# The second eviction and transpose of a left unit moved behind the sum and the mix of its segment

## The chip, the cores and the metric

The kernel runs on one core of one Trainium2 chip. The metric is the device time of one execution in microseconds; of three runs the median is 1787.72 us (1786.72 to 1793.3). All times below are microseconds of the device unless a unit is named. In the text PE is the matrix engine, DVE the vector engine, ACT the scalar engine, POOL the general-purpose engine, and SP the engine that, in the part of the kernel that matters here, issues every DMA.

## What is computed

Two branches are mixed by a gate, over one sequence of 2048 rows of 640 elements in bf16:

```
g = sigmoid((x * gate_w).sum(-1))
a: for s in range(64):                          # segments of 32 rows, in sequence
       h = concat([mem, x[32*s : 32*s+32]])     # 8 memory rows + 32 rows = 40
       q, k, v = h Wq, h Wk, h Wv               # 32 heads of 192
       p = softmax(mask(q k^T / sqrt(192)))
       o = (p v) Wo                             # 40 rows of 640
       mem = o[:8];  a[s] = o[8:]
b = (gelu(x w_gate) * (x w_up)) w_down
out = g * a + (1 - g) * b
```

The 64 segments are a recurrence: the first eight output rows of a segment are the memory of the next one, so no projection of the next segment can start before the sum of this one is transposed back.

## The kernel before

**Stages.** First comes branch b for all rows (until about 180 us), which also leaves x and b in DRAM scratch. Then come 64 segments of about 25 us each. They are all straight-line code: every engine has one list of instructions, written in the order in which the Python program records them, and a recording layer adds semaphore waits for each pair that touches the same memory. Nothing is reordered later, so each engine works through its list and a waiting instruction holds up all that stands behind it on that engine. For SP that means: a DMA whose data isn't ready holds up every DMA recorded after it.

**Main rows and left rows.** A segment has 40 rows. Only 32 of them fit a block of columns: the eight memory rows and the first 24 rows of x. The last eight x rows of each segment are called left rows. Those of four segments make 32 rows, a group; their Q and K don't depend on the memory, so they are projected ahead of time in `left units`. There is one unit for each group and octet of heads (8 heads; four octets): five steps `("lf", place, u, k)` of eight matmuls, one half for Q and one for K, into two PSUM banks. Then follow two eviction steps `("le", place, u, m)`, m = 0 for Q and m = 1 for K. `left_evac` makes of each: an ACT copy from PSUM to a row buffer (`left_rows`, L920), a DVE 32x32-block transpose of the row buffer into the store buffer `lst[3]` (L922), and after the K half one SP DMA of 192 KB from `lst[3]` to the scratch `left_qk_scratch` (`left_store`, L926). Later `stg_load` (L971) brings the left rows of a segment back, 96 KB at a time, and POOL copies them into the Q and K tiles (`left_fill`, L977 and L979).

**Places.** `PROGS` has one list of steps for each of the four segments of a group; segment s runs list s % 4, called its place here. Place 0 has one left unit, place 1 two, place 2 one, place 3 none (it has other extra work: the values of left rows, and the output projection of the left rows). The steps at the end of a list are `("pv", 3)`, the probabilities times the values for the last octet, and `("wo", 3, 0)`, `("wo", 3, 1)`, the last 48 matmuls (L1275) of the output projection.

**The end of a segment.** When the list is through, `segment` records, in this order: the two halves of the sum Z (DVE, L1429) each followed by its transpose back into the input tile of the next segment (DVE, L1433), then `mix` (DVE, L1021, with POOL's L1014 and L1019 ahead of it), then the deferred evictions (`post`), then `stg_load(s + 1, 1)` on SP. An `le` step whose position in its list is behind `("wo", 3, 1)` is deferred; the others are recorded where they stand:

```python
if n > n_wo:
    post.append(item[2:] + (n,))
else:
    left_evac(s, *item[2:], n)
...
mix(s)
...
for i in post:
    left_evac(s, *i)
...
    stg_load(s + 1, 1)
```

The position also picks the row buffer (`spare_rows`): ahead of `("wo", 3, 1)` it is the second value buffer for both halves, so the second ACT copy has to wait until the first transpose has read it; behind it, the row buffer lies in the K tile, which POOL's L979 of the next segment writes.

**Weights.** The weights don't all fit on chip. Sixteen slots of memory are shared by two pieces each: 13 of Q, K and V (384 KB) and three of Wo (480 KB). When PE has used a piece of the first octet, SP loads the piece of the last octet of the same segment over it (`swap_loads`, L630), in the order K piece 0, Q pieces 2 to 4, K pieces 1 to 4, V pieces 0 to 4, and three of Wo when `("wo", 0, 0)` and `("wo", 0, 1)` are through. The pieces are used in the same segment: Q and K of the last octet at about 10 to 15 us, V at 17 to 20, and Wo by the last 48 matmuls. The next segment swaps them back in the same way, so each segment loads 6.6 MB.

Of the kernel before, what the change touches and what calls it, by code (L numbers as in the profile page):

```python
# [231 lines left out]
def _build(nc, A_x, A_mem0, A_Wq, A_Wk, A_Wv, A_Wo, seg_len, w_gate, w_up, w_down,  # L232
# [271 lines left out]
    def piece_view(key, o):  # L504
        if key[0] == 3:
# [975 lines left out]
def bass_gated_mix__memory_aug_recurrent_mem_tr__glu_gated_geglu__prompt_kernel(  # L1481
    nc,
    A_x,
    A_mem0,
    A_Wq,
    A_Wk,
    A_Wv,
    A_Wo,
    A_seg_len,
    B_x,  # L1490
    B_w_gate,
    B_w_up,
    B_w_down,
    gate_w,
    out,
):
    _build(nc, A_x, A_mem0, A_Wq, A_Wk, A_Wv, A_Wo, A_seg_len, B_w_gate, B_w_up, B_w_down, gate_w, out)
# [33 lines left out]
```

## Time and profile before

| what | value |
|---|---|
| median of three runs | 1787.72 us |
| the profiled execution, its own time | 1784.35 us |
| its span, first to last instruction | 1782.5 us |
| granted clock of PE | 0.999 |
| PE busy | 1626.4 us, 91% |
| DVE, ACT, POOL busy | 54%, 45%, 18% |
| DMA | 500.22 MB, mean 281 GB/s |

The profiled execution is 3.4 us below the median of the runs.

The trace was cut at the end of the last L1275 matmul of each segment. The next table gives means over the segments of each place (segments 1 to 59; 14 of place 0 and 15 of each other). "Start" is the end of L1275 of the segment before, all times are from there, and a row tells of the segment that then runs.

| | place 0 | place 1 | place 2 | place 3 |
|---|---|---|---|---|
| segment time, start to the end of its L1275 | 24.91 | 25.46 | 23.59 | 25.89 |
| first projection matmul (L1092) | 0.67 | 0.64 | 1.11 | 1.47 |
| first weight load issued (K piece 0) | 1.21 | 3.07 | 1.67 | 2.13 |
| the same, landed | 4.53 | 6.71 | 5.54 | 5.77 |
| last V piece landed | 18.57 | 20.80 | 19.11 | 19.34 |
| last Wo piece landed | 22.46 | 25.01 | 22.81 | 23.10 |
| from there to the segment's end | 2.45 | 0.46 | 0.78 | 2.79 |

How to read it: what stands at the end of place 0's list shows in the column of place 1, and so on round; the column of place 0 follows the end of place 3, which has no left unit. In place 1 the end of the segment comes 0.43 or 0.44 us after the last Wo piece in 13 of 15 segments; in place 2 it comes at most 0.49 us after it in eight of 15.

### The profile page before, as it was taken

How to read it: one execution, taken by the hardware profiler on the slowest of the kernel's cores; microseconds unless marked ns; L12 is line 12 of the kernel's file. 1: busy time of each engine (PE TensorE's matmuls, PEld its weight loads, DVE VectorE, ACT ScalarE, POOL GpSimd, SP SyncE). 2: the span in 40 equal slices, each digit the busy share in tenths (PEclk: the TensorE clock that was granted, in tenths of full speed). 3: DMA queues.
4: the chain of work that ended last, by engine and by line, in shares of the span. 5: the costliest groups of instructions: out<-in, count | busy, mean ns of one | idle time of the engine just before them, and what ended most of it. 6: DMA issues, size and time to landing. Idle time of an engine off the chain costs nothing. (4 is left out here: it accounts for less than half of the span.)

```text
span 1782.5 us, 80354 instructions
## 1 busy us (share of the span) xinstructions
PE 1626.4 (91%) x39181; PEld 820.6 (46%) x31501; DVE 959.1 (54%) x2939; ACT 800.6 (45%) x1899; POOL 321.0 (18%) x1099
## 2 busy tenths in 40 slices
PE   9999989999899999898999999898989989898987
PEld 4554444444444444454444444454444444454444
DVE  2223655555565655555555655555555555555554
ACT  3222444544444444444444544444444444444443
POOL 1100111121111121111112112121212111111221
PEclk9999999999999999999999999999999999999999
DMA  9814887887778787888788886878778886888786
GB/s 322 292 48 166 314 303 255 321 292 285 278 285 316 278 306 258 306 305 299 273 277 294 310 307 247 311 274 324 272 267 292 299 291 237 313 294 304 270 299 243
DMA packets 265695, 500.22 MB, mean 281 GB/s; under 512 B 99688, under 2 KB 126592, under 8 KB 265344
## 3 DMA queue, kind: packets, MB, share of 16 engines
q1 hardware_dynamic: 262360, 492.03, 77.3%
q8 instruction: 276, 4.52, 1.0%
q10 hardware_dynamic: 2984, 3.05, 0.5%
q14 instruction: 75, 0.61, 0.1%
HBM read 473.88 MB, written 21.11 MB: 278 GB/s over the span
## 5 line engine op out<-in xcount | busy, mean ns | idle before, releaser
L1092 PE MATMUL ps<-arena 128*32 128x384 bf16 x9940 | 734.4, 328 | 61.4 <-DVE arena L1433 50.4
L226 PE MATMUL ps<-arena 128*32 128x384 bf16 x7680 | 586.7, 326 | 13.3 <-ACT arena L920 6.6
L1092 PEld LDWEIGHTS ps<-arena 128*32 128x32 bf16 x9940 | 255.5, 96 | 417.4 <-issue 254.1
L1126 DVE STREAM_TRANSPOSE arena<-arena 128x384 bf16<-128x384 bf16 x512 | 279.1, 564 | 230.6 <-ACT arena L1112 230.1
L1112 ACT ACTIVATE arena<-ps 128x384 bf16<-128x384 f32 x512 | 236.2, 489 | 180.2 <-PE ps L1092 171.9
L1252 PE MATMUL ps<-arena 128*32 128x320 bf16 x6144 | 295.8, 299 | 16.3 <-issue 16.2
L1252 PEld LDWEIGHTS ps<-arena 128*32 128x32 bf16 x6144 | 164.3, 96 | 76.8 <-issue 26.0
L1170 ACT ACTIVATE ps<-ps 104x160 f32<-104x160 f32 x256 | 74.1, 290 | 245.4 <-DVE ps L1160 245.4
L1158 DVE TENSOR_REDUCE arena<-ps 104x4 f32<-104x160 f32 x256 | 83.2, 325 | 187.0 <-PE ps L1146 187.0
L1208 ACT ACTIVATE arena<-ps 128x448 bf16<-128x448 f32 x192 | 104.8, 546 | 143.9 <-PE ps L1195 143.9
L977 POOL COPY arena<-arena 128x96 bf16<-128x96 bf16 x256 | 69.6, 272 | 535.2 <-PE ps L1146 427.2
L1242 POOL COPY arena<-arena 128x96 bf16<-128x96 bf16 x256 | 68.9, 269 | 496.5 <-ACT arena L1234 397.9
L1115 ACT ACTIVATE arena<-ps 128x384 bf16<-128x384 f32 x256 | 124.9, 488 | 63.2 <-PE ps L1092 63.1
L1234 ACT ACTIVATE arena<-ps 128x480 bf16<-128x480 f32 (+1 forms) x256 | 138.2, 540 | 28.4 <-PE ps L1225 23.6
L1223 PE MATMUL ps<-arena 128*64 128x160 bf16 x1536 | 121.9, 243 | 8.1 <-ACT arena L1115 1.0
L1223 PEld LDWEIGHTS ps<-arena 128*64 128x64 bf16 x1536 | 80.5, 109 | 94.5 <-ACT arena L1208 45.6
L915 PE MATMUL ps<-arena 128*32 128x384 bf16 x1280 | 111.5, 329 | 1.5 <-issue 1.3
L1225 PE MATMUL ps<-arena 128*64 128x64 bf16 x1536 | 104.7, 193 | 5.4 <-issue 5.4
L1172 DVE TENSOR_REDUCE arena<-ps 104x4 f32<-104x160 f32 x256 | 81.7, 319 | 51.6 <-ACT ps L1170 43.1
L922 DVE STREAM_TRANSPOSE arena<-arena 128x384 bf16<-128x384 bf16 x128 | 73.8, 577 | 58.8 <-ACT arena L920 55.5
L1160 DVE TENSOR_TENSOR ps<-ps,arena 104x160 f32<-104x160 f32 x256 | 85.1, 332 | 8.8
L1275 PE MATMUL ps<-arena 128*32 128x160 bf16 x3072 | 72.8, 234 | 13.1 <-DMA arena<-in_A_Wo_dram 7.2
(85 smaller groups left out, 1815.4 us busy)
## 6 DMA issues: line engine op xcount, KB each, us to landing
arena<-in_A_Wk_dram SPq DMA_DIRECT2D x335, 384.0 KB, 7.1
arena<-in_A_Wv_dram SPq DMA_DIRECT2D x335, 384.0 KB, 9.1
arena<-in_A_Wo_dram SPq DMA_DIRECT2D x205, 480.0 KB, 6.9
arena<-in_A_Wq_dram SPq DMA_DIRECT2D x209, 384.0 KB, 5.3
left_qk_scratch<-arena SPq DMA_DIRECT2D x64, 192.0 KB, 2.2
arena<-left_qk_scratch SPq DMA_DIRECT2D x126, 96.0 KB, 2.3
ffn_b_scratch<-arena ACTq DMA_DIRECT2D x16, 160.0 KB, 3.4
arena<-ffn_b_scratch SPq DMA_DIRECT2D x64, 40.0 KB
```

The lines of the kernel that those rows point to most:

```text
L226: return e.add_instruction(mybir.InstMatmult(name=nm, start_tensor_calc=like["start"], stop_tensor_calc=stop, tile_size=(128, 32), tile_po ...
L915: fns.append(lambda e, outp=outp, rhs=rhs, j=j: e.matmul(outp, lhs, rhs, start=(k == 0), stop=(k == KT - 1), tile_position=(0, 32 * j)))
L1092: fns.append(lambda e, outp=outp, rhs=rhs, j=j: e.matmul(outp, lhs, rhs, start=(k == 0), stop=(k == KT - 1), tile_position=(0, 32 * j)))
L1112: S_.add("act", lambda e, m=m, bk=bk: e.activation(out=rows_sb[m], in_=ps[:, bk, 0:384], func=ACTF.Copy), reads=[r_ps[bk]], writes=[r_rows ...
L1115: S_.add("act", lambda e, i=i, bk=bk: e.activation(out=v_sb[i % NVB].rearrange("p (c n) -> p c n", c=3), in_=ps[:, bk, 0:384].rearrange("p ...
L1126: S_.add("dve", lambda e: e.transpose(out=dst[:, :, 0:L], in_=rows_sb[m].rearrange("p (c r) -> p c r", r=L)), reads=[r_rows[m]], writes=[r ...
L1160: S_.add("dve", lambda e: e.tensor_tensor(out=S3, in0=S3, in1=mxb, op=ALU.subtract), reads=[rb, rst], writes=[rb], name="smax sub")
L1208: S_.add("act", lambda e: e.activation(out=PT, in_=ps[:, bank, 0:PTW + 128], func=ACTF.Copy), reads=[r_ps[bank]], writes=[r_PT], name="pT ...
L1223: return [lambda e: e.matmul(full, v[:, e0:e0 + 64], PTm[:, i], start=True, stop=False, tile_position=(0, 64 * i), skip_group_check=True), ...
L1225: lambda e: e.matmul(part, vl[:, e0:e0 + 64], PTl[:, i], start=False, stop=True, tile_position=(0, 64 * i), skip_group_check=True)]
L1234: S_.add("act", lambda e: e.activation(out=apx(u[:, 0, 0, :], [[R, na], [3 * R, 4], [1, R]]), in_=ps[:, A, 0:na * W].rearrange("p (c t r) ...
L1252: fns.append(lambda e, i=i, t=t, j=j, gv=gv: e.matmul(ps[32 * j:32 * j + 32, bank, 0:2 * DJ].rearrange("p (h n) -> p h n", h=2), lhs2[i], ...
```

## The change

At places 1 and 2 the step `("le", place, 1, 1)`, the eviction of the K half of the left unit u = 1, is moved behind `("wo", 3, 1)`, the last step of the list, where place 0 has it. Before, it stood ahead of both `wo` steps at place 1 and between them at place 2.

```diff
@@ place 1
-         ("wo", 2, 1), ("pv", 3), ("lf", 1, 1, 3), ("lf", 1, 1, 4), ("le", 1, 1, 0), ("le", 1, 1, 1), ("wo", 3, 0),
-         ("wo", 3, 1)],
+         ("wo", 2, 1), ("pv", 3), ("lf", 1, 1, 3), ("lf", 1, 1, 4), ("le", 1, 1, 0), ("wo", 3, 0), ("wo", 3, 1),
+         ("le", 1, 1, 1)],
@@ place 2
-         ("lf", 2, 1, 2), ("pv", 3), ("lf", 2, 1, 3), ("lf", 2, 1, 4), ("le", 2, 1, 0), ("wo", 3, 0),
-         ("le", 2, 1, 1), ("wo", 3, 1)],
+         ("lf", 2, 1, 2), ("pv", 3), ("lf", 2, 1, 3), ("lf", 2, 1, 4), ("le", 2, 1, 0), ("wo", 3, 0), ("wo", 3, 1),
+         ("le", 2, 1, 1)],
```

It takes effect in 15 groups (the last group has no left unit to prepare), so in 30 segments. In the program that comes of it, no instruction is added or taken away. PE, ACT, POOL and SP have their instructions in the same order as before. On DVE the transpose L922 of the K half now stands behind the two halves of Z, their transposes and the mix. The row buffer of that half changes to the one in the K tile, so its ACT copy no longer waits for the transpose of the Q half, and POOL's L979 of the next segment now waits for the moved transpose. The store L926 still stands on SP ahead of `stg_load` and of the next segment's weight loads, and still waits for the transpose.

## The prediction

> **What bounds the kernel now.** I read the page's first part, then who waits for whom, then the end of a place-0 and of a place-1 segment in the timeline, then the waits on the weight loads.
>
> PE is busy for 1626.4 of 1782.5 us at a granted clock of 0.999, so what there is to win lies in its pauses. The waits (waiter, releaser, total us, times, longest):
>
> ```profile
> PEld ps L1092 <- DVE arena L1433: 77.8, 126, 2.0
> ...
> DVE arena L922 <- ACT arena L920: 55.5, 90, 1.2
> ...
> PE ps L1092 <- DVE arena L1433: 50.4, 48, 1.8
> ...
> ACT arena L920 <- DVE arena L922: 24.4, 30, 1.1
> ```
>
> Those of L1092 are the pause at the 63 segment ends: the next projection waits for the transposed memory. The other two are the left unit's evictions waiting for each other, 30 times: the K half's copy for the Q half's transpose. Next the end of a place-1 segment, engine by engine (start, duration, engine, line; in brackets idle time and releaser):
>
> ```profile
> 828.02 0.39 PE L1275 MATMUL ps<-arena 128*32 128x160 bf16 x12 [0.17 <-DMA arena<-in_A_Wo_dram]
> ...
> 829.76 0.35 PE L1092 MATMUL ps<-arena 128*32 128x384 bf16 x4 [1.35 <-DVE arena L1433]
> ...
> 828.71 0.58 DVE L922 STREAM_TRANSPOSE arena<-arena 128x384 bf16<-128x384 bf16 x1 [0.68 <-ACT arena L920]
> 829.21 0.21 DVE L1429 TENSOR_TENSOR arena<-ps,arena 128x64 bf16<-128x64 f32 x1
> ...
> 829.32 0.37 SPq L926 DMA_DIRECT2D left_qk_scratch<-arena  x1
> 829.79 0.45 SPq L971 DMA_DIRECT2D arena<-left_qk_scratch  x1
> 830.31 0.42 SPq L630 DMA_DIRECT2D arena<-in_A_Wk_dram  x1
> ```
>
> PE ends at 828.42, but Z (L1429) starts only when the second L922 is through, at 829.21: 1.35 us of pause. The same end at place 0, which has the order that the change makes:
>
> ```profile
> 804.28 0.35 PE L1092 MATMUL ps<-arena 128*32 128x384 bf16 x4 [0.63 <-DVE arena L1433]
> ...
> 803.70 0.25 DVE L1429 TENSOR_TENSOR arena<-ps,arena 128x64 bf16<-128x64 f32 x1
> ...
> 804.89 0.57 DVE L922 STREAM_TRANSPOSE arena<-arena 128x384 bf16<-128x384 bf16 x1
> 806.58 1.04 DVE L1126 STREAM_TRANSPOSE arena<-arena 128x384 bf16<-128x384 bf16 x2 [1.12 <-ACT arena L1112]
> ...
> 805.49 0.38 SPq L926 DMA_DIRECT2D left_qk_scratch<-arena  x1
> 805.90 0.51 SPq L971 DMA_DIRECT2D arena<-left_qk_scratch  x1
> 806.45 0.45 SPq L630 DMA_DIRECT2D arena<-in_A_Wk_dram  x1
> ```
>
> The pause is 0.63, but against the segment's end (803.65) the store leaves at 1.84 and the first weight load at 2.80; in the place-1 case they leave at 0.90 and 1.89. Last, who waits for the weight loads (L630):
>
> ```profile
>   PEld ps L1092: 11.8, 22
>   PEld ps L1275: 11.7, 21
>   PE ps L1275: 7.2, 14
> ```
>
> So the loads already end last in some segments. The table of places in the profile section says where: in all of place 1 and half of place 2 the last Wo piece lands 0.43 to 0.49 us before the segment ends.
>
> **The change, part by part.** It acts in 30 segment ends, 15 of place 1 (the segment that follows runs place 2) and 15 of place 2 (then place 3).
>
> *Z and the memory transpose come earlier.* The first projection after places 1 and 2 now comes at 1.11 and 1.47 us (means); after place 0, with the new order, at 0.64. PE gains 0.47 and 0.83 us an end, at most 15 x 0.47 + 15 x 0.83 = 19.5 us. This is the whole of the gain.
>
> *The K half's copy and transpose.* The copy (ACT, 0.49 us) loses its wait for the Q half. The transpose (0.57) runs from 1.24 to 1.81 after the end, within DVE's idle time: 1.12 us are left over in the row of L1126 above. Both cost nothing; were that cover gone, the next Q and K transposes would start up to 0.57 later.
>
> *POOL.* L979 waits for the moved transpose. After place 0 it runs at 805.52 for 0.27 and the first score matmuls follow at 807.49, 1.7 us later. It costs nothing, as the L977 before it comes earlier too; a delay beyond that 1.7 would go to the scores one for one.
>
> *SP, the part that costs.* The store waits for the moved transpose. Behind it on SP stand the stage load L971, needed only at the third octet, and the sixteen weight loads. After place 0 the first weight load leaves at 3.07 us on average (2.8 where nothing else holds it), after places 1 and 2 now at 1.67 and 2.13. So the loads leave 1.40 and 0.94 us later against the segment's end, while PE wants them 0.47 and 0.83 us sooner. The loads are a stream without pause: in the trace undisturbed pieces land 0.97 us apart, and from the first to the last landing it takes 17.27 us in place 2. How far the later issue moves the landings isn't shown for places 2 and 3, so it is bounded. From below: place 3's first load leaves 0.92 later than place 0's and its last Wo piece lands 0.64 later, a share of 0.70; that makes 0.98 and 0.66. From above: place 1, the one place that has the new order ahead of it, lands its last V piece 1.69 and 1.46 later than places 2 and 3. Its first piece lands 1.17 and 0.94 later. I take the middle of what place 1 shows for first and last, 1.43 and 1.20, as it is the same mechanism and part of the upper figure may be place 1's own, with its second left unit.
>
> Place 2: the last Wo piece lands at 22.81 + 1.43 = 24.24, the segment ends 0.44 later (the tail where the loads bind) at 24.68, against 23.59 now: +1.09, times 15 = **+16.4 us**. Ends: 0.98 gives +0.64 or +9.6 us; 1.69 gives +1.35 or +20.3. PE's own path, 23.59 - 0.47 = 23.12, no longer decides.
>
> Place 3 has time at its end (2.79), but not in the middle: the trace has K pieces 2 and 3 of the last octet landing on average 1.28 and 1.21 us before PE uses them. PE 0.83 earlier and loads 1.20 later make 2.03; a wait of 2.03 - 1.21 = 0.82 opens and eats the 0.83: 15 x -0.01, **about 0**. Ends: 0.66 gives 0.83 + 0.66 - 1.21 = 0.28, net -0.55 or -8.3 us; 1.46 gives 1.08, net +0.25 or +3.8. The last Wo piece keeps 2.32 - 2.03 = 0.29.
>
> Places 0 and 1 keep what stands ahead of them: 0.
>
> Sum: 16.4 - 0.1 = **+16.3 us**, ends +1.3 and +24.1. Against the profiled execution's own 1784.35 that is 1800.6; this execution is 3.4 below the median of the runs, and on the median, 1787.72 + 16.3 = **1804.0 us**, slower by 0.9%.
>
> **A rule beside it.** What decides is whether the stream can go faster once it starts later. The rows: 12 x 384 KB and 3 x 480 KB, 6.19 MB, in 17.27 us are 359 GB/s, and 0.97 us a piece is 405 GB/s; the rest are hiccups that every place has. The Trainium skill, page "DMA: Bandwidth & Descriptors", section "Specifications", puts the fabric's ceiling at 435 GB/s; an estimate from that page is 14.2 us for those bytes. At this pace place 2's loads would land by 6.71 + 14.2 = 20.9 and bind nothing, and the sum would be the whole gain, -19.5 us, the first rival below taken to its end; by the rows it is +16.3. No segment of this trace comes near that pace.
>
> **The rivals.**
>
> *The loads still come in time, and it gets faster.* The place is the weight stream of place 2; it decides at a stream (first issue to last landing) of 23.59 - 0.44 - 3.07 = 20.08 us, below which place 2 gains. For it: early loads wait for PE to use the old pieces, and that part of the stream could close up; place 3 shows a share of 0.70 only. Against it: the stream is 21.14 us on average in place 2, 20.30 at the least, and 21.94 in place 1, where the loads leave late. Price: with landings where they are now, place 2 ends at 22.81 + 0.44 = 23.25, -0.34, and place 3 gains its 0.83 whole: 15 x -0.34 + 15 x -0.83 = -17.5, so 1770.2 us.
>
> *Gain and loss cancel.* The share of 0.70 holds: +1.3, 1789.0 us. For it: rows of two places in the same run. Against it: place 1 has the very order and shows more than the full shift.
>
> *The store gets into the stream.* It moves 192 KB out of idle DMA time into the first weight loads. Place 1 has such a store in mid-stream: its third Wo piece lands 1.81 after the second, place 2's 1.25 after, so 0.56 for a store. On top of 1.40 and 0.94 that makes 1.96 and 1.50: place 2 +1.62, place 3 0.83 + 1.50 - 1.21 - 0.83 = +0.29, times 15 = +28.7, 1816.4 us. Against it: after place 0 the store stands there already, and the first piece still lands 3.6 us after its issue, like the others.
>
> That the change does nothing is out: the order on DVE and the waits of store and copy differ in the built program.
>
> **How the numbers follow.** Half a per cent, 8.9 us, is about what a measurement of this kernel tells from no change. The forecast has a chance of 0.64, 0.08 of it below +8.9 us; the first rival 0.13 (0.01 of it within half a per cent), cancelling 0.13, the store in the stream 0.10. Slower: 0.56 + 0.10 = 0.66; within: 0.08 + 0.13 + 0.01 = 0.22; faster 0.12. The forecast's own range is that of the sum's ends, 1789 to 1812. For 8 in 10 it reaches to the cancelling case and to the store's, 1787 to 1816; what is left out is the faster rival and a little above.
>
> **What would show it.** PE's waits for L1433 should fall from 77.8 to about 58 us (77.8 - 19.5), and L920's waits for L922 should vanish; the first matmul after places 1 and 2 comes at 0.64, the store at 1.84, the first weight load at 2.8 to 3.1. PE's waits for L630 should about double. Place 2 takes 24.7 us with a tail of 0.44 in nearly all segments, place 3 25.9 with waits at its K pieces, places 0 and 1 what they take now. I am wrong if place 2's stream falls to 20 us, or if place 3's K pieces are still there when PE wants them.

## The result, and the profile after

The changed kernel takes a median of 1799.49 us against 1786.88 for the kernel before in the same series (eight runs each): a ratio of 1.0064, with a 95% interval of 1.004 to 1.0088, so slower by 0.6%, 12.6 us by the medians. The profiled execution took 1795.71 us, with a span of 1793.7; before it was 1784.35 and 1782.5.

The waits of the changed kernel (waiter, releaser, total us, times, longest), with those that answer to the lines shown of before. PEld is the load of a matmul's first operand into PE; in the lines below that is 32 columns of the segment's own rows and not a weight piece, but it stands ahead of its matmul, so a wait for a weight piece shows on PEld as well as on PE:

```profile
PEld ps L1092 <- DVE arena L1433: 58.1, 126, 0.9
...
PEld ps L1092 <- DMA arena<-in_A_Wk_dram: 45.4, 65, 2.3
...
DVE arena L922 <- ACT arena L920: 37.4, 66, 1.1
...
PEld ps L1092 <- DMA arena<-in_A_Wv_dram: 33.9, 54, 1.4
PE ps L1092 <- DVE arena L1433: 30.7, 48, 0.7
```

The pause at the segment ends fell from 77.8 to 58.1 us, as the change does it, and the longest from 2.0 to 0.9. The wait of L920 for L922 fell from 24.4 us in 30 waits to 6.4 in seven, a row further down in that view: of the 30, 25 stood at the ends of places 1 and 2 and are gone; the seven belong to the other left unit of place 1 (u = 0), which the change doesn't touch and which had five of the 30. In their stead stand waits of the projections for the K and V pieces, which came to 11.8 us in 22 waits on PEld before (79.2 in 119 now). The view of the weight loads (L630) says the same from the other side: who waited for them.

```profile
  PEld ps L1092: 79.2, 119
  PE ps L1092: 40.2, 65
  PEld ps L1275: 17.3, 28
  PE ps L1275: 11.4, 25
```

The end of the same place-1 segment that the prediction showed, engine by engine (start, duration, engine, line, idle time and releaser; this segment ends at 836.27):

```profile
835.87 0.39 PE L1275 MATMUL ps<-arena 128*32 128x160 bf16 x12 [0.56 <-DMA arena<-in_A_Wo_dram]
836.91 0.35 PE L1092 MATMUL ps<-arena 128*32 128x384 bf16 x4 [0.64 <-DVE arena L1433]
...
836.32 0.25 DVE L1429 TENSOR_TENSOR arena<-ps,arena 128x64 bf16<-128x64 f32 x1 [0.90 <-PE ps L1275]
...
837.51 0.58 DVE L922 STREAM_TRANSPOSE arena<-arena 128x384 bf16<-128x384 bf16 x1
...
838.11 0.37 SPq L926 DMA_DIRECT2D left_qk_scratch<-arena  x1
838.53 0.51 SPq L971 DMA_DIRECT2D arena<-left_qk_scratch  x1
839.08 0.45 SPq L630 DMA_DIRECT2D arena<-in_A_Wk_dram  x1
```

Z now starts 0.05 us after the end and PE goes on after 0.64; the moved transpose ends at 838.09, the store leaves at 1.84 from the end and the first weight load at 2.81, where they left at 0.90 and 1.89 before. By place, in means as in the table of before (15 segments; start is the end of the segment ahead):

| | place 1 | place 2 | place 3 |
|---|---|---|---|
| segment time, before / after | 25.46 / 25.32 | 23.59 / 24.67 | 25.89 / 25.73 |
| first projection matmul | 0.64 / 0.64 | 1.11 / 0.64 | 1.47 / 0.64 |
| first weight load issued | 3.07 / 2.98 | 1.67 / 3.23 | 2.13 / 2.93 |
| last V piece landed | 20.80 / 20.65 | 19.11 / 20.56 | 19.34 / 20.75 |
| last Wo piece landed | 25.01 / 24.86 | 22.81 / 24.23 | 23.10 / 24.46 |
| from there to the segment's end | 0.46 / 0.45 | 0.78 / 0.43 | 2.79 / 1.27 |

Place 0 stays at 24.9. In place 2 the last Wo piece now lands 0.43 or 0.44 us before the end in all 15 segments: loads set its end. 15 x 1.08 of place 2, 15 x -0.16 of place 3 and 15 x -0.14 of place 1 make 11.7 us, and the spans differ by 11.2.

### The profile page after: what moved, and what is told of

It is laid out like the page before. It is cut to its first block, busy times and chain, and to the rows that moved or that the text cites. A ratio compares the mean times of both kernels' runs of the same rounds, so it can differ in the third digit from the quotient of the medians.

```text
span 1793.7 us, 80324 instructions
## 1 busy us (share of the span) xinstructions
PE 1636.6 (91%) x39181; PEld 815.7 (45%) x31501; DVE 959.7 (54%) x2939; ACT 797.7 (44%) x1899; POOL 319.3 (18%) x1099
## 5 line engine op out<-in xcount | busy, mean ns | idle before, releaser
L1252 PE MATMUL ps<-arena 128*32 128x320 bf16 x6144 | 292.3, 302 | 7.4 <-issue 7.3
L1252 PEld LDWEIGHTS ps<-arena 128*32 128x32 bf16 x6144 | 162.3, 97 | 61.8 <-issue 12.4
L922 DVE STREAM_TRANSPOSE arena<-arena 128x384 bf16<-128x384 bf16 x128 | 73.5, 575 | 38.4 <-ACT arena L920 37.4
```

The lines of the kernel that those rows point to most:

```text
L1252: fns.append(lambda e, i=i, t=t, j=j, gv=gv: e.matmul(ps[32 * j:32 * j + 32, bank, 0:2 * DJ].rearrange("p (h n) -> p h n", h=2), lhs2[i], ...
```

## The experiments

The theory: the store waits on SP for the moved transpose, sixteen weight loads wait behind the store, and in places 2 and 3 the loads end last. Rivals: the moved transpose costs through POOL's L979; PE merely runs ahead of loads that come when they came; or the transposes' order is worth nothing. The kernel before took medians of 1778 to 1781 us on the chips of these series, less than the 1787 of the first series, so every kernel is given as its ratio to the runs of before of its own series. All eleven kernels had at least five runs. Their times by place are from one profiled execution each, which lay up to 9 us from the median of its kernel, so 0.2 us at a place can be chance (the two profiled executions of the changed kernel differ by 0.18 in place 2 and in place 3).

### The wait on SP alone

DVE and ACT keep the order of before; only the store waits for the mix as well (`r_bz` is what the mix writes, and `left_store` takes it as a further tile to wait for).

```diff
-        if m:
+        if m and u == 1 and s % 4 in (1, 2):
+            pend.append(unit(s, u))
+        elif m:
             left_store(*unit(s, u), 3)
...
         mix(s)
...
+        if pend:
+            left_store(*pend.pop(), 3, [r_bz])
...
         if s + 1 < NSEG:
             stg_load(s + 1, 1)
```

> The order on DVE and ACT is that of the kernel before; at places 1 and 2 only the store L926 is made to wait for the mix (L1021) as well, so it leaves at about the same time as in the changed kernel, and with it everything behind it on SP. Theory (the store holds up the weight loads): the first weight load of places 2 and 3 leaves at about 2.8 to 3.1 us instead of 1.67 and 2.13; place 2 gets 0.8 to 1.1 us longer, place 3, whose projections start no sooner, 0 to 0.2; in all 12 to 18 us slower than before (+0.7% to +1.0%), which is more than the changed kernel loses. Rival (the loss comes from PE running ahead of the loads, or from POOL's wait for the moved transpose, and SP has no part in it): within 3 us of before.

Measured 1.0097 [1.0077, 1.0118], 1796.83 against 1777.77 us. An end of place 1 in this kernel, where line numbers from 1344 on are four higher (L1433 is Z, L1437 its transpose); it ends at 837.72:

```profile
839.30 0.35 PE L1092 MATMUL ps<-arena 128*32 128x384 bf16 x4 [1.57 <-DVE arena L1437]
...
838.25 0.58 DVE L922 STREAM_TRANSPOSE arena<-arena 128x384 bf16<-128x384 bf16 x1 [0.63 <-ACT arena L920]
838.75 0.21 DVE L1433 TENSOR_TENSOR arena<-ps,arena 128x64 bf16<-128x64 f32 x1
...
839.63 0.34 DVE L1021 SCALAR_TENSOR_TENSOR arena<-arena 128x160 bf16<-128x160 bf16 x1
...
840.00 0.37 SPq L926 DMA_DIRECT2D left_qk_scratch<-arena  x1
840.42 0.51 SPq L971 DMA_DIRECT2D arena<-left_qk_scratch  x1
840.97 0.45 SPq L630 DMA_DIRECT2D arena<-in_A_Wk_dram  x1
```

The transposes stand as before, and the store's data is ready at 838.83, but the store leaves at 840.00, when the mix (L1021) is through. The first weight load comes at 2.99 on average in place 2, which takes 24.76 us, 1.17 more than before. So the wait on SP alone makes the whole loss and more; the rival without SP has fallen. Place 3 did not get longer, as I had expected, but shorter (25.57); its first projection comes at 0.98 instead of 1.47, which the next experiment explains.

### One place at a time

The change at place 1 alone, and at place 2 alone.

> The change at place 1 alone. Theory: place 2, the segment after it, loses what it lost in the changed kernel, 1.08 us, and nothing else moves: +16 us (+0.9%). Rival (a cost of the moved transpose itself, the same at both places): half the loss of the changed kernel, about +6 us.

> The change at place 2 alone. Theory: place 3 starts 0.83 us sooner and gives nearly all of it back at the K pieces of the last octet, as in the changed kernel: -2 us, within 4 us of before. Rival (a cost of the moved transpose itself, the same at both places): about +6 us.

Place 1 alone: 1.0048 [1.003, 1.0066], 8.5 us by the ratio. Place 2 alone: 0.9991 [0.9977, 1.0006]. The loss is all place 1's, which is the segment of place 2; a cost of the transpose itself, alike at both, is out. But the change at place 1 alone loses only half of the 16 us that I expected. Place 2 does take 24.51 us, 0.92 more than before (23.51 in the kernel with place 2 alone, on the same chip). What I had not seen is that place 3 gains though nothing was changed at its head: it takes 25.31, its first projection comes at 1.02 (1.47 before) and its first load at 1.69 (2.13). While PE waits for Wo at the end of place 2, ACT and DVE go on with the left unit: its second transpose ends 0.55 us after the segment's end, against 0.99 before. A late end hides part of the next pause.

### The whole change once more

> The changed kernel as it is, on the chip and beside the runs of before that the experiments had, so that the parts can be added up on one chip. Theory: the sum of place1_only (+0.48%) and place2_only (-0.09%), so +0.2% to +0.7%. Rival (the two places work on each other): outside that.

1.0082 [1.0068, 1.0097]; this series ran on another chip than the two parts. It is above their sum, 0.39%, and above the upper end that I gave, though the first series of the same kernel, 0.64% [0.40, 0.88], is not clear of that sum. That the places work on each other is seen in the traces, by the way just told: with place 1 changed, the pause ahead of place 3 is down to 1.02 already, so the change at place 2 wins 0.38 us there and not 0.83, and still pays for the later loads: place 3 takes 25.55 here (25.73 in the first series) against 25.31 with place 1 alone.

### POOL's wait

The deferred K half gets back the row buffer that it had, so that L979 does not wait for the moved transpose.

```diff
-    def left_evac(s, u, m, n):
-        left_rows(*unit(s, u), m, lb[u, m], lst[3], r_lst[3], *spare_buf(spare_rows(PROGS[s % 4], n)))
+    def left_evac(s, u, m, n, buf=None):
+        left_rows(*unit(s, u), m, lb[u, m], lst[3], r_lst[3], *spare_buf(spare_rows(PROGS[s % 4], n) if buf is None else buf))
...
-            left_evac(s, *i)
+            left_evac(s, *i, 1 if q else None)
```

> The changed kernel, but the deferred K half of places 1 and 2 keeps the row buffer that it had before (the second value buffer), so POOL's L979 of the next segment does not wait for the moved transpose, while its ACT copy waits for the first transpose again. Theory (SP alone): as slow as the changed kernel, +0.5% to +0.8% against before, place 2 at 24.6 us. Rival (POOL's wait costs part of it): at least 0.3% better than the changed kernel.

1.0053 [1.0035, 1.0071], place 2 at 24.39 us with its first load at 3.21. The 24.39 is from the fastest of its twelve runs, 9 us below their median, and the ratio is 0.1% below the changed kernel's first one and 0.3% below its second, so the times alone don't rule out a small part. The trace does for the first scores: L979 now ends 1.78 us after the start of place 2 and not 2.20, yet the first product of Q and K (L1141) starts at 4.04 in both kernels. A few tenths of a per cent anywhere else are not ruled out.

### The store behind the V loads

The stores of places 1 and 2 are kept back as above, and sent in the next segment:

```diff
             swap_loads(s, item)
+            if item == ("g", 1, KT - 1) and pend:
+                left_store(*pend.pop(), 3)
```

> The changed kernel, but the two stores of places 1 and 2 are recorded on SP behind the last V load of the next segment, so no weight load waits for the moved transpose. Theory: the pause stays 0.64 us, the first weight load of places 2 and 3 leaves at about 1.2 to 1.6; place 2 gains 0.4 to 0.8 us against before and place 3 its 0.83 whole: 18 to 24 us faster than before (-1.0% to -1.3%), about 30 us faster than the changed kernel. Rival (POOL's wait, the row buffer, or PE running ahead of the loads): as slow as the changed kernel, +8 to +15 us.

> DVE and ACT in the order of the kernel before, the two stores of places 1 and 2 moved behind the last V load as in late_store_12. It differs from late_store_12 by the changed order of the transposes alone, with the loads free in both. Theory: in late_store_12 place 2 was held by its last Wo loads and place 3 by PE, so the order is worth little in place 2 (0 to 0.2 us) and its 0.83 us in place 3: this kernel is 13 to 16 us slower than late_store_12, about 4 us slower than before (0 to +0.4%). Rival (the gain of late_store_12 comes from the loads alone and the order of the transposes is worth nothing): as fast as late_store_12, -0.7%.

With the changed order: 0.9933 [0.9913, 0.9952]. With the order of before: 1.0011 [0.9992, 1.003]. Freeing the loads turns the changed order from a loss of 0.6% into a gain of 0.7%, but it is less than the 1.0 to 1.3% that I expected. The first load of place 2 does leave at 1.18, yet place 2 takes 23.65 us, no less than before (this is the slowest of its six runs, 7 us above their median, so the true figure may be lower): the store now stands in mid-stream, and the first Wo piece lands 1.81 us after the last V piece (1.23 before), which gives back 0.58. Place 3, with 2.4 us in hand at its end, keeps its gain (25.26). The second kernel, slower by 0.8% than the first, shows that the gain is the order's: moving these stores alone wins nothing. Part of what the order gives is the loads' own start: in the second kernel they leave at 1.71 and 1.68 us and not at 1.18, because the first load follows the first projection by about 0.54 us wherever nothing else holds it (1.17 and 1.14 here, 0.64 in the first kernel).

### The store early in the stream, and on the queue of ACT

The first is the kernel of the section above with all three places and `("g", 0, 3)` for the position, behind the third weight load. The other leaves the store where it was and lets ACT issue it, at all three places and, in a second version, at places 1 and 2 alone:

```diff
-            left_store(*unit(s, u), 3)
+            left_store(*unit(s, u), 3, "act" if u == 1 else None)
```

> The changed kernel, with the store of all three places recorded on SP behind the third weight load of the next segment, so that the transpose is long done when SP comes to it. Theory: the first weight load leaves at 1.2 us after each end; place 1 loses its wait for loads (0.5 to 1.2 us less than 25.3), place 2 comes near 23.4, place 3 near 25.2; the store takes up to 0.58 us of the stream. In all 15 to 30 us faster than before (-0.9% to -1.7%). Rival: no faster than late_store_12 (-0.7%), if place 1 is held by something other than the late loads.

> The changed kernel, with the store of all three places issued by ACT, recorded where it was. SP no longer waits for the transpose; ACT does, in its idle time after the segment's end, and issues at about 1.84. Theory: loads as in early_store_012, and the 192 KB move while the first loads are still on their way: 20 to 32 us faster than before (-1.1% to -1.8%). Rival (ACT's issue delays its next row copies, which the first scores need): no faster than early_store_012, with the first scores later by what the issue takes.

> The changed kernel with the stores of places 1 and 2 issued by ACT, place 0 left as it was: the change with the wait on SP taken out of it and nothing else improved. Theory: place 2 as in act_store_012 (23.2 us, -0.4), place 3 too (25.1, -0.8), place 1 as before (25.4): 15 to 20 us faster than before (-0.8% to -1.1%), and slower than act_store_012 by the 0.9 us of place 1 times 15. Rival (most of the gain of act_store_012 is place 0's): within 0.3% of before.

> The order of the kernel before, with the stores of all three places issued by ACT. It differs from act_store_012 by the changed order of the transposes alone, with the loads leaving at 1.2 to 1.7 us in both. Theory: the order is worth 0.8 us at place 3 and 0.2 to 0.5 at place 2, so this kernel is 14 to 20 us slower than act_store_012 (-0.5% to -0.9% against before). Rival (with the loads free the order is worth nothing): as fast as act_store_012, -1.7%.

| kernel | ratio to before [95%] | place 1, 2, 3, us |
|---|---|---|
| early in the stream, all places | 0.9858 [0.9836, 0.988] | 24.51, 23.25, 25.12 |
| on ACT, all places | 0.9834 [0.981, 0.9857] | 24.56, 23.21, 25.06 |
| on ACT, places 1 and 2 | 0.9894 [0.9876, 0.9913] | 25.18, 23.15, 25.12 |
| on ACT, all places, order of before | 0.9963 [0.995, 0.9976] | 24.47, 23.60, 25.87 |

The end of place 1 with the store on ACT (it ends at 816.09):

```profile
816.73 0.35 PE L1092 MATMUL ps<-arena 128*32 128x384 bf16 x4 [0.64 <-DVE arena L1433]
...
816.14 0.32 SPq L971 DMA_DIRECT2D arena<-left_qk_scratch  x1
817.27 0.33 SPq L630 DMA_DIRECT2D arena<-in_A_Wk_dram  x1
...
817.93 0.37 ACTq L926 DMA_DIRECT2D left_qk_scratch<-arena  x1
818.43 0.87 ACT L1112 ACTIVATE arena<-ps 128x384 bf16<-128x384 f32 x2 [2.67 <-PE ps L1092]
```

The stage load no longer waits behind the store, the first weight load leaves at 1.18, and the store goes out at the same 1.84 without holding up either. ACT's next row copy comes at 2.34, as it did after place 0 in the kernel before (805.98 - 803.65 = 2.33), so the delay that the rival named is not there. Its median of 1751.71 us against 1780.61 is the lowest of all, 1.7% faster than before and, by the two ratios to before, some 2.3% faster than the changed kernel. What the changed order is worth with the loads free is the distance of the last row from the second: 1.3%, where the pause was 0.64 instead of 1.59 and 1.57 us. The lesser half of the gain is place 0's: 0.6% between the second and the third row. Both distances compare ratios of two series on two chips; by the places of the profiled executions the order wins 0.39 us in place 2 and 0.81 in place 3, 18 us or 1.0%.

The last row misses what I expected of it (-0.5% to -0.9%): it is 0.4% faster than before. I had the loads leave at 1.2 to 1.7 us in both kernels; with the order of before they leave at 2.13 and 2.12 in places 2 and 3, again 0.54 behind the first projection. So the 1.3% is the pause and the earlier start of the loads together. The store early on SP and the store on ACT can't be told apart by their times (medians of 1753.91 and 1751.71, intervals that overlap).

## Why the prediction was right

**Forecast.** 1804.0 us was said, slower by 0.9%, with a range of 1787 to 1816; measured were 1799.49 and +0.64%, +12.6 us where +16.3 was said. The likeliest case is the one that happened, by the mechanism that was named.

**The pause.** Right: 0.64 us after both places, and 58.1 us of waits against about 58. The waits of L920 for L922 were to vanish and did so where the change acts; the forecast had counted all 30 there, and five were of the other left unit, where 6.4 us remain. The pause was said to be the whole of the gain; the kernel with the store on ACT and the order of before bears this out, as its places 2 and 3 take 23.60 and 25.87 us, no less than before.

**SP, the part that costs.** Right. The store leaves at 1.84 and the first load at 3.23 and 2.93 on average; the kernel with nothing but this wait is 1.0% slower than before. The landings moved by 1.45 (V) and 1.42 (Wo) in place 2, where 1.43 was taken as the middle between two rows; in place 3 by 1.41 and 1.36, where 1.20 was taken. Place 1, the place that had the order already, was the right row to go by, and in place 3 its upper figure, 1.46, was the nearer one. That the middle hit place 2 to 0.01 us is luck: it was picked from a range of 0.98 to 1.69. A smaller slip: the last Wo piece binds in 13 of the 15 segments of place 1 and not in all.

**Place 2.** +1.09 us foretold, +1.08 measured; 16.4 and 16.2 us.

**Place 3.** "About 0" was foretold, -0.16 us a segment came: -2.4 us instead of -0.1. The K pieces did bind, as said: the trace of after has pieces 2 and 3 landing 0.10 and 0.18 us ahead of their use, where it was 1.28 and 1.21. The wait that opens was sized 0.82; with the larger shift (1.47 and 1.40 for pieces 2 and 3, where 1.20 was taken) PE reaches piece 3 at 14.43, 0.36 later than before. The step that failed is that this stays lost until the segment's end: 0.52 us came back. The forecast also left the last Wo piece only 0.29 us ahead of its use; once the wait has eaten PE's gain, its own figures make 2.32 - 1.20 = 1.12, and 0.80 was measured. Part of what came back is seen in the matmuls of Wo (L1252), in the page's groups of before and then of after (matmuls and weight loads; busy us, mean ns, idle before, what ended it):

```profile
L1252 PE MATMUL ps<-arena 128*32 128x320 bf16 x6144 | 295.8, 299 | 16.3 <-issue 16.2
L1252 PEld LDWEIGHTS ps<-arena 128*32 128x32 bf16 x6144 | 164.3, 96 | 76.8 <-issue 26.0
```

```profile
L1252 PE MATMUL ps<-arena 128*32 128x320 bf16 x6144 | 292.3, 302 | 7.4 <-issue 7.3
L1252 PEld LDWEIGHTS ps<-arena 128*32 128x32 bf16 x6144 | 162.3, 97 | 61.8 <-issue 12.4
```

The idle time for which the profile shows no releaser ("issue") more than halved over the whole program, from 16.2 to 7.3 us ahead of the matmuls. Of this, 7.5 us before and 1.9 after lie in place 3, so it gave back 5.6 us there, 0.37 of the 0.52 us a segment. Why it shrinks behind the new waits stays open.

**Place 1** was taken as unchanged. Its mean fell by 0.14 us, 2.1 us in all. In the nine profiled executions other than before's that leave the head of place 1 alone (the changed kernel's two among them) it lies between 25.10 and 25.41, so the 25.46 of the profiled execution of before is probably a high draw, and these 2.1 us no part of the change. In the two profiled executions the two terms together make up the distance from 16.3 to about 12 us.

**The waits for L630** were said to double. They rose fourfold: from 23.5 (11.8 + 11.7) to 96.5 us (79.2 + 17.3) on PEld. The lost time was sized well, but the waits took the place of other ones, so their sum is no measure of the loss.

**The rivals.** *The loads still come in time*: it decided at a stream below 20.08 us, and place 2's is 21.00, 20.37 at the least. A later start did not close it up. *Gain and loss cancel*: the share of 0.70 did not hold: the last Wo piece moved by 1.42 for 1.56 us of later issue in place 2, a share of 0.91, and by 1.36 for 0.80 in place 3, 1.70. *The store gets into the stream*: partly. The first piece lands 0.96 us later than before in place 2 (6.50 against 5.54) and 0.89 in place 3 (6.66 against 5.77), the last V piece 1.45 and 1.41, so half a microsecond comes in between. That the store, just ahead of the first load, is the cause isn't shown, and one run speaks against it: in the kernel with the late store no store lies in that stretch of place 2, and it still takes 13.64 us (5.09 to 18.73), about the 13.56 of the kernel with the change at place 1 alone, on the same chip, where the store stands ahead. In mid-stream, in the kernel with the late store, it does take 0.58, near the 0.56 of this rival's price. But the whole shift stayed below its 1.96 and 1.50. From first to last landing place 2 takes 17.73 us after (6.50 to 24.23), 349 GB/s, no faster than the 359 of before. The fabric ceiling of 435 GB/s that the Trainium skill states, page "DMA: Bandwidth & Descriptors", section "Specifications", left room for a faster stream; no run here contradicts it, but the stream did not use the room.

## What to carry to other kernels

A step that is moved off one engine's path takes its DMA along: ask what stands behind that DMA on its queue before counting the gain. Here the move was worth 1.0 to 1.3% with the loads free, and a store of 192 KB that waited at the head of a queue of weight loads turned it into a loss of 0.6%; issuing the store from an engine that idles at that moment spared the loss and kept the gain. Where a kernel has several places with the same step in different orders, the place that has the new order already shows what follows it: the segment behind it, not only its own end, is the row to read.

## What the runs showed of the hardware that was not expected

A stream of loads that is late hides pauses of other kinds. In the kernel before, with the loads of place 1 late, the pause ahead of place 2 was 1.11 us; with the same order and the loads freed (the store on ACT) it was 1.59, since the left unit's transposes no longer had the time of PE's wait for Wo. So single changes don't add up here: +0.48% and -0.09% apart, +0.64% and +0.82% in the two series of both together, of which the second is clear of the sum.

PE's busy time rose from 1626.4 to 1636.6 us with the same 39181 matmuls, at a granted clock of 0.996 against 0.999. If busy time went with the clock, 0.3% would make about 5 us of it, an estimate from these two figures. The other profiles don't bear out a simple link: 1624 to 1637 us at 0.995 or 0.996, 1616 to 1633 at 0.997 to 0.999. Where the rest is from was not tried.
